# A strided-attention and feed-forward kernel on one core: fewer and finer loads at the start, and one more block of tokens in the seven-product form

## The chip, the cores and the metric

The kernel runs on one core of a Trainium2 chip, the other cores being idle. The metric is the time of one execution on the device, in microseconds (us): the median of three executions was 305.05 us (304.64 to 305.45). The profiled execution that all views below come from took 306.2 us by the same clock; its trace spans 304.4 us from the first to the last instruction. The clock that TensorE was granted is full (1.000) throughout.

Engines: TensorE multiplies matrices (PE in the profile; PEld is its loading of weights), VectorE is DVE, ScalarE is ACT, GpSimd is POOL, SyncE is SP. GpSimd issues the loads, because these also convert float32 to float16; SyncE issues stores and the transposes that are done by DMA.

## The reference, cut to what matters

```python
q, k, v: (8, 8, 576, 64)            # batch, heads, positions, head dimension
scores = (1 / 8) * q @ k.T          # for each batch and head
rel = pos[:, None] - pos[None, :]
mask = (0 <= rel < 32)                        # heads 0 to 3, "local"
mask = (rel >= 0) & (rel % 32 == 0)           # heads 4 to 7, "strided"
attn = softmax(where(mask, scores, -1e9))
x = (attn @ v) as (4608, 512)       # tokens x (heads * head dimension)
h = x @ w_in                        # w_in (512, 2048)
g = s * relu(h) ** 2 + b
out = g @ w_out                     # w_out (2048, 512), out float32
```

A local head needs only bands of 96 positions with the 32 before them, a strided head only 72 x 72 squares of eight interleaved classes each, so the attention is small. The two feed-forward products are large: 4608 x 512 x 2048 and 4608 x 2048 x 512.

## The kernel before

The program is fully unrolled. While it is being built, a small planner (`Plan`) keeps a clock of its own, with estimated durations and landing times, and picks for TensorE at each moment the next piece of work that it believes ready: a step of the attention, of the first feed-forward product (`ff1`), or of the second (`ff2`). The engines then execute in that order and wait on semaphores where reality is later than the plan. Estimates therefore change nothing but the order.

```python
LAT = {"A": 70.0, "V": 70.0, "P": 70.0, "D": 12000.0, "X": 7000.0, "Y": 12000.0}  # ns, added to an end
...                                        # A, V, P: ACT, DVE, POOL;  D, X, Y: transposes and stores by DMA

def load_vl(b):                            # v of the four local heads of batch b
    vl = v_loc[b % NV]
    for h in range(4):
        nc.gpsimd.dma_start(out=vl[LPAD:128, h, :, 0:D], in_=v_band(b, h))

def load_w_in():                           # pieces of 512, 512 and 1024 columns
    wv = moe_w_in.rearrange("(c p) f -> p c f", p=128)
    for i, at in enumerate((0, 512, 1024)):
        nc.gpsimd.dma_start(out=w_in_sb[i], in_=wv[:, :, at:at + w_in_sb[i].shape[2]])
...
def mu(eng):                               # division by the sum of the softmax, after P times v
    if eng == "A":
        for i in range(per):               # per = 6 (local) or 4 (strided)
            nc.scalar.activation(out=st["x"][:, j0 + i, 64 * e:64 * e + 64],
                                 in_=st["pa", e, j][0:nq, i, 0:D], func=AF.Copy,
                                 scale=st["rec", e, j][0:nq, i])
        return
    nc.vector.tensor_tensor(out=st["x"][:, j0:j0 + per, 64 * e:64 * e + 64],
                            in0=..., in1=..., op=ALU.mult)
...
def trans(name, j, group): ...             # q and k of a pair of heads transposed on TensorE (L429, L437)
x_by_dma = b >= 2 if loc else XS_DMA <= b < B - 1    # else x is transposed on TensorE (xtrans, L662)
...
def ff1(T, ft, ct, ...):                   # block T of 512 tokens: 16 ft x 4 ct matmuls of 512 columns (L907)
    needs.append(("w_in", ft // 4))        # relu to u on ACT or DVE, then square to gT

def ff2(T, ts, ft, ...):                   # plain form: 4 ts x 16 ft matmuls of 512 columns (L965)
    needs=[("g", T, ft), ("w_out", ft // 4)]

def ff2_seven(T):                          # T >= SEVEN = 3: seven products of 16 matmuls, 256 columns (L875)
    ...                                    # sums of quarters of gT on DVE (L747), quarters of w_out
                                           # combined once (w_mix), results joined on DVE (L794, L806, L817)
...
def second(eng):                           # everything of batch 1, after w_in, on GpSimd's queue
    fetch_qk(1)
    load_vl(1)
    ...
    early_v(1)                             # v of the strided heads
    weights_out(range(4))                  # w_out in four pieces
...
def keep_running(until):                   # matmuls on a tile of ones where the plan has nothing ready
    ghz = 1.2 if plan.t < 6000 else 2.4    # (L1201)
```

The seven-product form takes a block's 512 x 2048 times 2048 x 512 as a 2 x 2 by 2 x 2 product of quarters: seven products of quarters instead of eight, with additions in exchange. Blocks 0 to 2 take the plain form, blocks 3 to 8 the seven-product form.

Of the kernel before, what the change touches and what calls it, by code (L numbers as in the profile page):

```python
# [15 lines left out]
class Plan:  # L16
# [7 lines left out]
    LAT = {"A": 70.0, "V": 70.0, "P": 70.0, "D": 12000.0, "X": 7000.0, "Y": 12000.0}  # L24
# [92 lines left out]
class Step:  # L117
    def __init__(self, fn, ns, needs=(), group=None, keys=(), posts=(), after=None):
        self.fn, self.ns, self.needs, self.group = fn, ns, needs, group
        self.keys, self.posts, self.after = keys, posts, after  # L120
# [3 lines left out]
def kernel(  # L124
# [32 lines left out]
    for p in range(SQ):  # L157
        for c in range(SQ):
# [30 lines left out]
               for i, n in enumerate((512, 512, 1024))]  # L189
# [123 lines left out]
    def load_vl(b):  # L313
        vl = v_loc[b % NV]
        for h in range(4):
            nc.gpsimd.dma_start(out=vl[LPAD:128, h, :, 0:D], in_=v_band(b, h))  # L316
# [8 lines left out]
    def load_w_in():  # L325
        wv = moe_w_in.rearrange("(c p) f -> p c f", p=128)
        for i, at in enumerate((0, 512, 1024)):
            nc.gpsimd.dma_start(out=w_in_sb[i], in_=wv[:, :, at:at + w_in_sb[i].shape[2]])
# [80 lines left out]
    def pair_steps(b, m):  # L409
# [10 lines left out]
        def trans(name, j, group):  # L420
            alone = loc and b < HEAD_T

            def f():
                if j == 0:
                    st["p" + name] = bank(group).bitcast(FP16)[:, 0:S]
                if alone:
                    for e in range(2):
# [12 lines left out]
            s = Step(f, 70 if alone else 35, needs=[("in", name + sfx, b, mm)],  # L440
                     group=group if j == 0 else None)
            if j == nt - 1:
                key = ("t", name, id_)
                s.keys = [key]
                if name == "q":
# [14 lines left out]
                    s.posts = [([key], {"A": 1190, "V": 1440 if loc else 918}, g,  # L460
# [17 lines left out]
        x_by_dma = b >= 2 if loc else XS_DMA <= b < B - 1  # L478
# [128 lines left out]
        def av(e, j, group):  # L607
# [13 lines left out]
            if j % per == per - 1:  # L621
# [10 lines left out]
                def mu(eng):  # L632
                    if eng == "A":
                        for i in range(per):
# [12 lines left out]
                                                 **({"A": 225.0 * per} if b == 0 else {})}, mu,  # L647
# [67 lines left out]
    SEVEN = 3  # L715
# [45 lines left out]
    def mix_post():  # L761

        wl, wr = [[w_out_sb[:, H * j:H * j + H, 256 * k:256 * k + 256] for j in range(2)]
                  for k in range(2)]
        jobs = ((3, wr[1], wr[0]), (1, wr[0], wl[0]), (2, wr[1], w_mix[1]), (4, wl[1], w_mix[2]))
        before = [("F2", SEVEN - 1)]
        for i, x, y in jobs:
            plan.post(before, {"V": 1250.0},
                      lambda eng, i=i, x=x, y=y: nc.vector.tensor_tensor(
                          out=w_mix[i], in0=x, in1=y, op=ALU.subtract), [("w_mix", i)])  # L770
            before = [("w_mix", i)]
        plan.post([("ev", SEVEN - 1, ts) for ts in range(4)], {"V": 350.0},
                  lambda eng: nc.vector.tensor_tensor(
                      out=bcs[:, 256:512], in0=bcs[:, 256:512], in1=bcs[:, 0:256],
                      op=ALU.subtract), [("dbc",)])
# [121 lines left out]
    def ff1(T, ft, ct, group, cts=(0, 1, 2, 3), early=False):  # L897
        tok0 = T * PS
        def f():
            if ft == 0 and ct == cts[0]:  # L900
                gts[T] = gp.tile([128, NFT, PS], FP16, tag="gT", name="gT")
            if ct == cts[0]:
                gts["h", T, ft] = bank(group)
            at = tok0 % (NX * S)
            n = min(PS, NX * S - at)
            for lo, hi in ((0, n), (n, PS))[:1 + (n < PS)]:
                nc.tensor.matmul(  # L907
                    out=gts["h", T, ft][:, lo:hi],
                    lhsT=w_in_sb[min(ft // 4, 2)][:, ct].rearrange(
                        "p (c x l) -> p c l x", x=128, l=4)[:, max(ft // 4 - 2, 0), ft % 4],  # L910
                    rhs=xT[ct][:, (at + lo) % (NX * S):(at + lo) % (NX * S) + hi - lo],
                    start=(ct == cts[0] and lo == 0), stop=(ct == cts[-1] and hi == PS))
# [109 lines left out]
    def landing(cost):  # L1022

        nonlocal ring
        ring = max(ring, plan.t + 2000.0) + cost

        return ring + (6000.0 if plan.t > 60000.0 else 600.0)
# [4 lines left out]
    def fetch_qk(b):  # L1032
# [6 lines left out]
        for name in ("q", "k"):  # L1039
# [3 lines left out]
            if b < HEAD_T:  # L1043
                arrive(both(name + "l", b), landing(1500))
                continue
            plan.done["raw", name, b] = landing(1700 if b > 1 else 1450)
            for mm in range(2):
                pair_post(b, name, mm, ("raw", name, b))
        for name in ("qs", "ks"):
            arrive(both(name, b), landing(2000 if b > 1 else 1750))  # L1050
# [12 lines left out]
    def early_v(b):  # L1063
# [3 lines left out]
        plan.done["raw", "v", False, b] = landing(1800)  # L1067
# [5 lines left out]
    def after_landing(i, src):  # L1073
# [7 lines left out]
    AT = {"ql0": 5700.0, "kl0": 6800.0, "ql1": 7900.0, "kl1": 8900.0, "qs": 10100.0,  # L1081
          "ks": 11600.0, "vs": 13600.0, "vl0": 7100.0, "vl1": 14700.0}
# [5 lines left out]
    after_landing(0, loaded[0, "ql"][0:1, NL // 2:NL // 2 + 1])  # L1088
# [4 lines left out]
    def weights_in(eng):  # L1093
# [5 lines left out]
        for keys, cost in ([0], 2700), ([1], 2500), ([2, 3], 5000):  # L1099
# [12 lines left out]
    def second(eng):  # L1112
# [3 lines left out]
        plan.done["raw", "vl", 1] = landing(3200)  # L1116
# [5 lines left out]
    plan.post(both("vl", 0) + both("vs", 0) + [("w",)], {"P": 14000.0}, second, [("free",)])  # L1122
# [12 lines left out]
    for b in range(B):  # L1135
        for m in range(4):
            steps, last_av = pair_steps(b, m)
            att.append(steps)
            if b + 2 < B:

                if m == 0:
# [7 lines left out]
                    [("fetch", b + 2)] + both("vs", b), {"P": 3600.0}, lambda eng: fetch_v(b + 2),  # L1149
# [3 lines left out]
    for T in range(NBLK):  # L1153
# [26 lines left out]
        for ts in range(4):  # L1180

            parts = 2 if T == NBLK - 1 and ts == 3 else 1
            for part in range(parts):
                gr = Group("f2", F2B)
                for ft in range(NFT):
                    f2.append(ff2(T, ts, ft, gr, part, parts))
                    f2[-1].pos = T + 0.25 + (ts + (part + ft / NFT) / parts) / 4
    def keep_running(until):

        ghz = 1.2 if plan.t < 6000 else 2.4  # L1190
# [26 lines left out]
    while i2 < len(f2) or any(at_i[p] < len(att[p]) for p in range(len(att))):  # L1217
# [5 lines left out]
        active = [p for p in range(first, min(first + 4, len(att))) if at_i[p] < len(att[p])]  # L1223
        for p in active:
# [67 lines left out]
```

## Time and profile before

| | |
|---|---|
| median of three executions | 305.05 us |
| span of the trace | 304.4 us |
| TensorE, DVE, ACT, POOL busy | 97%, 71%, 60%, 33% of the span |
| start of `ff1` of blocks 0, 1, 2, 3 | 18.97, 56.98, 90.76, 116.84 us |
| first matmul of `ff2` of block 0, last matmul of all | 40.81, 301.0 us |

A line of the groups gives the source line, the engine and operation, the tiles out<-in with shape and count, then busy us and mean ns of one, then the idle time just before. A line of the stages ("A:B ...") gives, for each engine, busy us and number of instructions, then TensorE's clock, the share of the DMA engines and GB/s. A line of the timeline gives start, length, engine, line, and in brackets how long the engine had been idle and what ended that. Landing times of single transfers are those of the trace, too.

### The profile page before, as it was taken

What the parts mean: (1) busy time and instruction counts of PE and PEld (TensorE: products, weight loads), DVE (VectorE), ACT (ScalarE), POOL (GpSimd) and SP (SyncE); (2) the same over time, 40 slices, a digit from 0 to 9 for tenths busy, and PEclk for the clock granted to TensorE, in tenths of its full rate; (3) what the DMA queues carried; (4) which work ended last, traced back from release to release, by engine and by line L of the source; (5) the groups of instructions that cost most, each with busy time, mean ns of one, the idle gap of its engine ahead of it and who ended that gap; (6) DMA issues with size and microseconds to landing.
All of it is one profiled execution on the core that took longest, in us unless ns stands there. A gap on an engine that the chain in (4) does not pass through costs nothing.

```text
span 304.4 us, 6800 instructions
## 1 busy us (share of the span) xinstructions
PE 296.4 (97%) x2674; PEld 205.8 (68%) x2674; DVE 216.6 (71%) x474; ACT 183.9 (60%) x330; POOL 99.3 (33%) x146
## 2 busy tenths in 40 slices
PE   8998999999999999999999999999999999999995
PEld 3764655666555568767567776778888666766784
DVE  6665897698966688737997698777765366737563
ACT  2966963898747677478585946695725445445300
POOL 8771753930961095029502961200000000000000
PEclk9999999999999999999999999999999999999999
DMA  8999999999999699999999999944010200300123
GB/s 136 183 201 202 137 213 190 179 198 149 83 160 165 98 100 149 132 186 147 142 153 172 142 160 159 155 105 131 14 37 34 72 34 0 106 0 2 69 82 126
DMA packets 100826, 37.29 MB, mean 122 GB/s; under 512 B 80907, under 2 KB 97803, under 8 KB 100795
## 3 DMA queue, kind: packets, MB, share of 16 engines
q0 software_dynamic: 57232, 18.08, 60.1%
q1 hardware_dynamic: 43562, 18.78, 33.3%
q8 instruction: 21, 0.34, 0.5%
q14 instruction: 11, 0.08, 0.1%
HBM read 36.86 MB, written 10.32 MB: 155 GB/s over the span
## 4 chain that ended last, share of the span: by engine, by line
PE 83%; DMA 8%; DVE 3%; POOL 3%; issue 1%; ACT 1%; POOLq 0%
PE ps_f L907 36%; PE ps_f L875 20%; PE ps_f L965 12%; DMA kl<-in_k_dram 5%; PE ps_s L557 3%; PE ps_a L614 3%; DMA vs<-in_v_dram 2%; PE ps_s L875 2%; DMA xT<-x_dram 1%; PE ps_t L875 1%; PE ps_s L965 1%; PE ps_t L614 1%; PE ps_t L662 1%; PE ps_t L437 1%; PE ps_f L437 1%
## 5 line engine op out<-in xcount | busy, mean ns | idle before, releaser
L907 PE MATMUL ps_f<-xT,w_in_sb 128*128 128x512 f16 (+4 forms) x696 | 148.1, 340 | 0.0
L934 ACT ACTIVATE u<-ps_f 128x512 f16<-128x512 f32 x137 | 80.8, 595 | 72.6 <-PE ps_f L907 69.9
L907 PEld LDWEIGHTS <-w_in_sb 128*128 128x128 f16 x704 | 71.7, 113 | 33.1 <-DMA w_in_sb<-in_moe_w_in_dram 0.5
L875 PEld LDWEIGHTS <-gT 128*128 128x128 f16 x512 | 49.0, 98 | 12.5 <-issue 0.4
L965 PE MATMUL ps_f<-w_out_sb,gT 128*128 128x512 f16 x176 | 47.6, 379 | 0.0
L875 PE MATMUL ps_f<-w_out_sb,gT 128*128 128x256 f16 x312 | 44.2, 273 | 0.3 <-DVE o L806 0.3
L944 DVE TENSOR_TENSOR gT<-u 128x1024 f16<-128x1024 f16 x46 | 32.1, 697 | 15.1 <-ACT u L934 14.4
L942 ACT ACTIVATE gT<-u 128x1024 f16<-128x1024 f16 x26 | 27.5, 1057 | 0.7
L640 DVE TENSOR_TENSOR x_nat<-ps_a,rec 72x256 f16<-72x256 f32 (+1 forms) x55 | 25.3, 459 | 0.9
L316 POOL DMA_DIRECT2D v_loc<-in_v_dram x28 | 20.7, 759 | 14.3 <-DMA w_in_sb<-in_moe_w_in_dram 6.0
L965 PEld LDWEIGHTS <-gT 128*128 128x128 f16 x192 | 17.0, 98 | 11.1
L575 ACT ACTIVATE p_str<-ps_s 72x432 f16<-72x432 f32 (+1 forms) x45 | 20.1, 481 | 4.7 <-PE ps_s L557 4.6
L575 ACT ACTIVATE p_loc<-ps_s 128x384 f16<-128x384 f32 x46 | 20.8, 494 | 2.2 <-PE ps_s L557 1.8
L614 PEld LDWEIGHTS <-p_str 72*128 72x128 f16 x256 | 15.3, 98 | 7.3 <-issue 0.4
L747 DVE TENSOR_TENSOR gT<-gT 128x1024 f16<-128x1024 f16 x28 | 18.5, 683 | 1.4 <-ACT gT L942 1.3
L875 PE MATMUL ps_f<-w_mix,gT 128*128 128x256 f16 x144 | 19.3, 273 | 0.0
L875 PEld LDWEIGHTS <-S 128*128 128x128 f16 x160 | 15.5, 98 | 3.7
L629 DVE RECIPROCAL rec<-ps_a 72x4 f32<-72x4 f32 (+1 forms) x55 | 9.7, 177 | 11.2 <-PE ps_a L614 11.0
L321 POOL DMA_DIRECT2D v_str<-in_v_dram x16 | 13.0, 816 | 9.6 <-PE ps_f L907 5.6
L583 DVE TENSOR_TENSOR p_loc<-p_loc,masks 128x1152 f16<-128x1152 f16 x14 | 10.5, 750 | 7.6 <-ACT p_loc L575 7.4
L875 PE MATMUL ps_f<-w_mix,S 128*128 128x256 f16 x96 | 13.4, 273 | 0.0
L976 DVE SCALAR_TENSOR_TENSOR o<-ps_f,s_sb,bcs 128x512 f32<-128x512 f32 x11 | 8.2, 749 | 6.4 <-PE ps_f L965 6.2
(162 smaller groups left out, 413.2 us busy)
## 6 DMA issues: line engine op xcount, KB each, us to landing
out_dram<-o SPq DMA_DIRECT2D x34, 256.0 KB, 3.4
w_out_sb<-in_moe_w_out_dram POOLq DMA_DIRECT2D x4, 512.0 KB, 9.4
v_loc<-in_v_dram POOLq DMA_DIRECT2D x28, 72.0 KB, 8.5
qs<-in_q_dram POOLq DMA_DIRECT2D x6, 288.0 KB, 6.6
ks<-in_k_dram POOLq DMA_DIRECT2D x6, 288.0 KB, 8.0
ql<-in_q_dram POOLq DMA_DIRECT2D x5, 288.0 KB, 9.7
kl<-in_k_dram POOLq DMA_DIRECT2D x16, 72.0 KB, 3.8
v_str<-in_v_dram POOLq DMA_DIRECT2D x16, 72.0 KB, 9.9
```

The source lines that it names most:

```text
L316: nc.gpsimd.dma_start(out=vl[LPAD:128, h, :, 0:D], in_=v_band(b, h))
L321: nc.gpsimd.dma_start(out=vs[:, h, :, 0:D], in_=v[b, 4 + h].rearrange("(p j) d -> p j d", j=ST))
L575: nc.scalar.activation(out=st["pw", g][0:nk, 0:2 * n * nq], in_=st["s", g][0:nk, 0:2 * n * nq], func=AF.Exp, scale=scale)
L614: nc.tensor.matmul(out=st["a"][:, j % per, :], lhsT=st["pw", g][0:nk, i * nq:i * nq + WIDE], rhs=vt[0:nk, 2 * mm + e, j, :])
L640: nc.vector.tensor_tensor(out=st["x"][:, j0:j0 + per, 64 * e:64 * e + 64], in0=st["pa", e, j][0:nq, 0:per, 0:D], in1=st["rec", e, j][0:nq, ...
L747: nc.vector.tensor_tensor(out=at(out), in0=at(x), in1=at(y), op=op)
L875: nc.tensor.matmul(out=gts[name, T, t][:, 0] if halves else gts[name, T][:, t], lhsT=lhs(k, t), rhs=rhs(k), start=fresh and k == 0 and (ha ...
L907: nc.tensor.matmul(out=gts["h", T, ft][:, lo:hi], lhsT=w_in_sb[min(ft // 4, 2)][:, ct].rearrange("p (c x l) -> p c l x", x=128, l=4)[:, ma ...
L934: nc.scalar.activation(out=u, in_=gts["h", T, ft], func=AF.Relu)
L942: nc.scalar.activation(out=g, in_=u, func=AF.Square)
L944: nc.vector.tensor_tensor(out=g, in0=u, in1=u, op=ALU.mult)
L965: nc.tensor.matmul(out=gts[id_], lhsT=gts[T][:, ft, ts * 128:(ts + 1) * 128], rhs=w_out_sb[:, ft, cols], start=(ft == 0), stop=(ft == NFT ...
```

## The change

Its parts, by what they are for:

- **Loads.** `load_vl` brings v of the four local heads in one transfer instead of four, so that GpSimd issues fewer; w_in comes in four pieces of 512 columns, so that the last half needn't land whole before it is used.
- **First batch.** The planner's table of landing times (`AT`) and other estimates for the first two batches are replaced by others; its clock starts at 1850 ns; transposes of batch 0 that have begun go first (`sticky`); the second half of the first v is requested when the first piece of q lands, not the second.
- **Seven products from block 2 on** (`SEVEN` 3 to 2). The combinations of w_out are formed in another order, so that three of the four can be formed before block 1 is done.
- **Divisions on ScalarE** become a choice for every batch, not for batch 0 alone.
- **Last batch.** The strided heads' x of batch 7 is transposed by DMA too.
- **Estimates** of transposes by DMA and of later landings are lowered (`LAT`, `landing`).

The diff, cut to its core:

```diff
-    LAT = {"A": 70.0, "V": 70.0, "P": 70.0, "D": 12000.0, "X": 7000.0, "Y": 12000.0}
+    LAT = {"A": 70.0, "V": 70.0, "P": 70.0, "D": 10000.0, "X": 6500.0, "Y": 6000.0}
...
-               for i, n in enumerate((512, 512, 1024))]
+               for i, n in enumerate((512, 512, 512, 512))]
...
     def load_vl(b):
-        vl = v_loc[b % NV]
-        for h in range(4):
-            nc.gpsimd.dma_start(out=vl[LPAD:128, h, :, 0:D], in_=v_band(b, h))
+        nc.gpsimd.dma_start(
+            out=v_loc[b % NV].rearrange("p h t d -> p (h t) d")[LPAD:128, :, 0:D],
+            in_=v.rearrange("b h (t p) d -> b p (h t) d", p=LQ)[b, :, 0:4 * LT])
...
-            s = Step(f, 70 if alone else 35, needs=[("in", name + sfx, b, mm)],
+            s = Step(f, 40 if alone else 35, needs=[("in", name + sfx, b, mm)],
                      group=group if j == 0 else None)
+            s.sticky = b == 0 and j > 0
...
-        x_by_dma = b >= 2 if loc else XS_DMA <= b < B - 1
+        x_by_dma = b >= 2 if loc else XS_DMA <= b
...
-                                                 **({"A": 225.0 * per} if b == 0 else {})}, mu,
+                                                 "A": 260.0 * per}, mu,
...
-    SEVEN = 3
+    SEVEN = 2
...
-        jobs = ((3, wr[1], wr[0]), (1, wr[0], wl[0]), (2, wr[1], w_mix[1]), (4, wl[1], w_mix[2]))
-        before = [("F2", SEVEN - 1)]
+        early = [("bcs",)] + ([("F2", SEVEN - 2)] if SEVEN > 1 else [])
+        jobs = ((3, wr[1], wr[0], ALU.subtract, early), (2, w_mix[3], wl[0], ALU.add, []),
+                (4, wl[1], w_mix[2], ALU.subtract, []),
+                (1, wr[0], wl[0], ALU.subtract, [("F2", SEVEN - 1)]))
...
-        return ring + (6000.0 if plan.t > 60000.0 else 600.0)
+        return ring + (3500.0 if plan.t > 60000.0 else 600.0)
...
-    AT = {"ql0": 5700.0, "kl0": 6800.0, "ql1": 7900.0, "kl1": 8900.0, "qs": 10100.0,
-          "ks": 11600.0, "vs": 13600.0, "vl0": 7100.0, "vl1": 14700.0}
+    AT = {"ql0": 5200.0, "kl0": 6500.0, "ql1": 7750.0, "kl1": 8550.0, "qs": 10150.0,
+          "ks": 11650.0, "vs": 13400.0, "vl0": 7100.0, "vl1": 12000.0}
...
-    after_landing(0, loaded[0, "ql"][0:1, NL // 2:NL // 2 + 1])
+    after_landing(0, loaded[0, "ql"][0:1, 0:1])
...
-        for keys, cost in ([0], 2700), ([1], 2500), ([2, 3], 5000):
+        for keys, cost in ([0], 2700), ([1], 2500), ([2], 2500), ([3], 2500):
...
-    plan.post(both("vl", 0) + both("vs", 0) + [("w",)], {"P": 14000.0}, second, [("free",)])
+    plan.post(both("vl", 0) + both("vs", 0) + [("w",)], {"P": 12500.0}, second, [("free",)])
...
+    plan.t = 1850.0
+
     def keep_running(until):
-        ghz = 1.2 if plan.t < 6000 else 2.4
+        ghz = 1.2 if plan.t < 6400 else 2.4
...
+        active.sort(key=lambda p: not att[p][at_i[p]].sticky)
```

Left out are further estimates of the same kind (landings of q, k and v of batch 1, durations of two copies, GpSimd's time for a load) and the renaming that four pieces of w_in need in `ff1`.

## The prediction

> **What bounds the kernel now.** I read the page first, engine shares and the row of slices:
>
> ```profile
> PE 296.4 (97%) x2674; PEld 205.8 (68%) x2674; DVE 216.6 (71%) x474; ACT 183.9 (60%) x330; POOL 99.3 (33%) x146
> ...
> PE   8998999999999999999999999999999999999995
> ...
> DMA  8999999999999699999999999944010200300123
> ...
> L965 PE MATMUL ps_f<-w_out_sb,gT 128*128 128x512 f16 x176 | 47.6, 379 | 0.0
> ```
>
> TensorE is full in nearly every slice. But the last line shows why that share can't be taken as it stands: one 512-column matmul is said to last 379 ns. In the timeline the same matmuls *start* every 215 to 216 ns, so records overlap and small gaps hide behind them. I therefore took the start-to-start steps from the trace: 215.7 ns for 512 columns (L907, L965), 109.3 ns for 256 (L875), 32 ns for a 72-column transpose (L662). Summing what every step exceeds its form's usual step, I find 1.4 to 2.4 us in each ten us up to 50 (part of it an artefact of transposes that run in pairs), then about 0.1 us in each ten us up to the end, with one exception of 0.47 us at 177. So there are two regimes: up to about 57 us the order of landings decides; after it TensorE is simply full, and only fewer columns help. By stages:
>
> ```profile
> 18.90:26.90 8.00, 7.88 (x47) 4.14 (x47) 4.56 (x8) 5.09 (x11) 1.96 (x5) 1.00 1.18 208
> 26.90:31.30 4.40, 2.34 (x35) 1.24 (x36) 2.02 (x3) 2.89 (x4) 1.44 (x2) 1.00 1.54 190
> 31.30:40.80 9.50, 9.50 (x120) 6.59 (x121) 8.65 (x19) 8.53 (x19) 8.34 (x12) 1.00 1.23 158
> ...
> 57.00:150.00 93.00, 93.00 (x812) 59.60 (x811) 68.90 (x169) 66.91 (x125) 44.04 (x63) 1.00 1.28 144
> ```
>
> The hole is in the second row. The list of waits names it:
>
> ```profile
> PE ps_t L429 <- DMA ql<-in_q_dram: 1.4, 1, 1.4
> ...
> PE ps_t L429 <- DMA kl<-in_k_dram: 0.6, 1, 0.6
> ```
>
> and TensorE's timeline shows what stood before it in order:
>
> ```profile
> 23.00 4.05 PE L907 MATMUL ps_f<-xT,w_in_sb 128*128 128x512 f16 x18
> 28.49 0.45 PE L429 MATMUL ps_t<-ident,ql 96*64 96x96 f16 x12 [1.44 <-DMA ql<-in_q_dram]
> ```
>
> By start-to-start steps these two holes are 1.61 and 0.78 us. At 26.9 exactly half of block 0's first product was done, 32 of 64 matmuls. The other half needs the 1024-column piece of w_in, which landed at 26.60; the plan put q of batch 1 first, and it landed at 28.44. On GpSimd's queue:
>
> ```profile
> 22.06 0.75 POOL L316 DMA_DIRECT2D v_loc<-in_v_dram  x1 [1.96 <-DMA w_in_sb<-in_moe_w_in_dram]
> 26.89 0.72 POOL L316 DMA_DIRECT2D v_loc<-in_v_dram  x1 [4.08 <-DMA w_in_sb<-in_moe_w_in_dram]
> 28.73 0.73 POOL L316 DMA_DIRECT2D v_loc<-in_v_dram  x1 [1.11 <-DMA ql<-in_q_dram]
> 31.47 0.72 POOL L316 DMA_DIRECT2D v_loc<-in_v_dram  x1 [2.01 <-DMA kl<-in_k_dram]
> ```
>
> Each of the four v transfers is held until the transfer eight issues earlier has landed (w_in at 21.49 and 26.60, ql at 28.44, kl at 31.18). So w_out goes out only at 33.63; its first piece lands at 40.16, and the second product of block 0 starts at 40.81.
>
> **What the Trainium skill says.** "TensorE: Matmul & The Clock Gate", section "Back-to-back issue gap", gives N/2.4 + 2.5 ns, thus 215.8 and 109.2 ns for 512 and 256 columns; the trace agrees with 215.7 and 109.3. "Perfetto Trace Analysis", section "Identifying the Most-Contended Engine", calls matmul busy time a bad measure because matmuls are pipelined; here 379 against 215.7 ns. "DMA: Bandwidth & Descriptors", section "Rules for kernel authors", says to coalesce many small transfers, while its section "Why small descriptors are slow (HBM only)" puts the cost on each descriptor. A v row arrives as 128 bytes, whether in one transfer or four. The trace agrees that these are slow: between 32 and 34 us, while they arrive, 70 GB/s move, against 199 to 218 from 18 to 30. Thus I credit the merged transfer with its issues, not its bytes.
>
> **The change, part by part.**
>
> *Seven products for block 2.* Removed: 64 matmuls x 215.7 ns = 13.80 us. Added: 112 x 109.3 = 12.24 us. TensorE saves 1.56 us, in the regime where it is full, so all of it counts. DVE pays: 8 sums x 0.683 (row L747) = 5.5 us, and 7 joins x 0.75 + 0.69 against 4 x 0.75 plain ones, +2.9 us; together +8.4 us. The four combinations of w_out only move earlier. DVE was busy 28.8 of 40 us from 110 to 150, where block 2's second product now lies; 37 of 40 would be too tight.
>
> *Divisions on ScalarE.* This is what the choice is for: a division costs DVE 0.414 us (strided) or 0.546 us (local), and ACT some 0.9 to 1.35 us (12 small ones took 2.7 us, 0.225 each). ACT was busy 27.6 of those 40 us. Moving about ten divisions brings DVE back to some 32 of 40. Worth nothing by itself on TensorE; it protects the 1.56 us.
>
> *Batch 7's x by DMA.* Removed: 16 transposes x 32 ns = 0.51 us of TensorE, and two copies. Batch 7 was done near 219 us, and block 7, the first that needs it together with batch 6, started at 236.99, so a round trip through DRAM of some 15 us in the plan is covered. All 0.51 us counts.
>
> *w_in in four pieces, better estimates, merged v.* At a landing pace of 2.6 us a piece (18.93 to 21.49 for the second) the third piece should land near 24.1 and the fourth near 26.6. TensorE needs 16 x 0.2157 = 3.45 us for what one piece feeds. It thus stays behind the landings from 18.9 on and never waits for w_in; the holes of 1.61 and 0.78 us get filled with the second half of `ff1`. One 512-column matmul on ones at 20.4 (0.4 us) goes as well. What of batch 0's attention ran after 18.97 (transposes of x, some 0.8 us) can lie before, as v's second half is requested about 2.5 us earlier. Sum of what could be gained: 1.61 + 0.78 + 0.4 + 0.8 = 3.6 us. Work up to `ff2` of block 0 would then end near 40.8 - 3.6 = 37.2.
>
> But `ff2` needs w_out, and DMA is the limit here. v of batch 1 is now one issue that can leave after the third piece of w_in, and v strided and w_out follow without three more holds. I estimate the first piece of w_out 1 to 1.5 us earlier, at 38.7 to 39.2: the bytes ahead of it are the same, and only the thin stretch around 32 us can be closed. Attention of batch 1 fills part of the remaining one to two us. I credit 2.5 of the 3.6 us.
>
> *The first 6 us.* The planner's clock starting at 1850 ns removes about five 427 ns matmuls on ones, so the first transposes can start at 5.3 rather than 6.37. I give nothing for this: `ff1` cannot start before w_in lands, at 18.93, and its request waits for q of the strided heads (landed 10.15), which doesn't move.
>
> *Lower estimates for DMA* remove no work. They move steps of TensorE nearer to the true landings. The plan allowed 12 us for a transpose by DMA that landed after 2.6 to 10.6; I subtract 0.5 us of new waits.
>
> Sum: 1.56 + 0.51 + 2.5 - 0.5 = 4.07 us. 305.05 - 4.07 = 301.0 us.
>
> **The rivals.** *w_out takes the place of the wait for q.* For it: the DMA row is 8 or 9 from the start to slice 25, so moving TensorE ahead only brings it to the next landing sooner. Against it: attention of batch 1 is at hand, and DMA has a thin stretch to close. If w_out doesn't move at all, the start gives some 1 us, and the time is 302.5.
>
> *DVE becomes the bound at block 2.* For: it was busy 9.5 of 10 us from 150 to 160 already. Against: ACT has room, and block 3 ran the same form in 149 to 177 with only 0.47 us lost. If it happens, the 1.56 us are lost and the time is 302.6 or more.
>
> *Plan too optimistic.* Two transposes of x through DRAM landed at 167.3 and 173.2, and block 5 started at 179.1; with 6 us less in the plan it might be placed at about 173, right at the landing. If each of five blocks waited 0.5 us, the time would be 303.
>
> *All goes well*: the whole 3.6 us, half a microsecond from the early start, no new waits: 305.05 - 1.56 - 0.51 - 4.1 = 298.9.
>
> **Range and chances.** The two savings in columns, 2.07 us, are nearly certain; the start is the uncertain term, between 1 and 4 us, less 0 to 2 us of new waits. That gives 299.2 to 303.2 for 8 in 10. 2% of 305.05 is 6.1 us; faster than 298.95 needs everything: 0.09. Slower by that much would need a stall of over 10 us: 0.02. Within 2%: 0.89.
>
> **What would show it.** The seven-product step: L965 at 128 matmuls instead of 192, L875 at 784 instead of 672, still 109 ns apart, and no waits of TensorE on DVE between 110 and 150. Divisions: L635 on ACT after 57 us. Batch 7: L662 at 88 instead of 104. The start: no wait on ql or kl of batch 1; `ff1` of block 0 in one run from about 18.9; `ff2` starting at 38.5 to 39.2, with any hole before it ended by w_out; block 1 starting near 54.5. The optimistic plan: waits of TensorE on transposes by DMA after 100 us. The prediction is wrong if w_in's first piece moves from 18.9, if `ff2` of block 0 still starts after 40, or if TensorE loses over 1 us after 60.

## The result, and the profile after

The changed kernel takes 313.92 us (median of four executions, 313.09 to 314.86), beside 304.85 us for the kernel before on the same chip: the ratio is 1.0296, with a 95% interval of 1.0262 to 1.0331. It is 9 us slower, where the prediction had it 4 us faster. The profiled execution took 313.09 us; its trace spans 311.0 us, against 304.4 before. (The spans differ by 6.5 us and not by 9.1: the profiled execution was the fastest of four after, and before it took 306.2 us, over its median.)

First the page of the kernel after: busy times, then the row of TensorE in 40 slices of 7.8 us, its granted clock and the DMA engines, then one group of matmuls and the loads of v; the last line is that of the kernel before.

```profile
PE 296.5 (95%) x2703; PEld 211.3 (68%) x2703; DVE 218.2 (70%) x470; ACT 200.0 (64%) x400; POOL 86.0 (28%) x122
...
PE   6999999999999999999958999899999999999994
...
PEclk9799999999999999999996999999999999999998
DMA  8999999997999799999999999814310210200213
...
L968 PE MATMUL ps_f<-w_out_sb,gT 128*128 128x512 f16 x112 | 29.9, 379 | 0.6 <-DVE u L939 0.6
...
v_loc<-in_v_dram POOLq DMA_DIRECT2D x7, 288.0 KB, 12.4
...
v_loc<-in_v_dram POOLq DMA_DIRECT2D x28, 72.0 KB, 8.5
```

The busy time of TensorE is the same as before to 0.1 us, which means nothing here, as the records overlap. The row of slices says more: one large hole, a 5 and an 8 in slices 21 and 22 (155.5 to 171 us), with a 6 for the clock in the second of them. One hole of some microseconds near 160 us, then, in a stretch in which the kernel before was full. The 8 in slice 26 is a smaller one. (The 7 of the clock in slice 2 is 3.4 us of half clock from 8.6 to 12.0.) The last two lines give the median time from issue to landing of v's loads: 12.4 us, and 8.5 for the four smaller transfers of before.

By stages (columns: length, busy time of PE, PEld, DVE, ACT and POOL with their instructions, granted clock, DMA share, GB/s), of the kernel after:

```profile
26.90:31.30 4.40, 4.40 (x42) 2.22 (x41) 2.02 (x4) 3.57 (x7) 1.58 (x3) 1.00 1.68 188
...
57.00:150.00 93.00, 93.00 (x875) 65.22 (x874) 75.95 (x174) 77.51 (x167) 35.86 (x50) 1.00 1.46 140
160.00:170.00 10.00, 5.71 (x35) 3.86 (x35) 3.60 (x7) 3.87 (x8) 1.76 (x4) 0.66 1.16 194
```

and the last of these stretches in the kernel before:

```profile
160.00:170.00 10.00, 10.00 (x79) 7.61 (x78) 5.76 (x10) 6.24 (x13) 4.78 (x9) 1.00 1.14 171
```

The hole at 26.9 to 31.3, on which most of the prediction's working was spent, is closed: TensorE is busy for all of the 4.40 us, against 2.34. The block with more work for VectorE, 57 to 150, is full. What is lost is lost at 160 to 170: 35 matmuls instead of 79, and a mean clock of 0.66. TensorE's waits of the kernel after (in total, how many, longest):

```profile
PE ps_s L558 <- DMA kT_loc<-kl: 4.7, 1, 4.7
PE ps_a L429 <- DMA kl<-in_k_dram: 1.2, 1, 1.2
...
PE ps_s L558 <- DMA kT_alt<-kl: 0.7, 1, 0.7
PE ps_t L429 <- DMA ql<-in_q_dram: 0.6, 1, 0.6
```

(those on kl and ql are batch 0's, at 6.9 and 5.0 us), and its timeline around the longest:

```profile
159.32 0.27 PE L879 MATMUL ps_f<-w_mix,gT 128*128 128x256 f16 x1
164.29 0.82 PE L558 MATMUL ps_s<-qD_loc,kT_loc 128*128 128x192 f16 x4 [4.70 <-DMA kT_loc<-kl]
164.91 0.64 PE L879 MATMUL ps_f<-w_mix,gT 128*128 128x256 f16 x2
165.34 1.06 PE L911 MATMUL ps_f<-xT,w_in_sb 128*128 128x512 f16 x2
```

The scores of batch 6 (L558) stand next in TensorE's order and need the transpose of k by DMA, which lands near 164.2. Behind them stand 512-column matmuls that need nothing of it, but the order was fixed when the program was built. Then comes a second loss that no list of waits has: from 162.2 to 169.0 the trace grants half the clock, and the 512-column matmuls start every 427 ns instead of 216. The Trainium skill, page "TensorE: Matmul & The Clock Gate", Part 1, "What's actually happening", says that one idle window of about 3.4 us brings the half clock, and that one busy window is needed to leave it. Here it lasted 6.8 us, two such windows, after a wait of 4.87 us by start-to-start steps; of the 3.4 us before it TensorE was idle for 2.6, so a window need not be idle throughout.

Summing what each start-to-start step exceeds its form's usual one, as the prediction did, the stretch 150 to 170 lost 7.3 us, against 0.1 before; 190 to 210 lost 1.2 (most of it a wait for another transpose of k), against 0.1; and the end comes 4.5 us after the start of the last matmul instead of 3.5. Against these 9.3 us stand 2.1 us of columns saved, 0.3 us that TensorE is ahead at 60 us, and 0.5 us of the wait at 177 of before, which is gone. That leaves 6.4; the spans differ by 6.5.

### The profile page after: what moved, and what is told of

Same layout as the page of the kernel before. It is cut to its first block, busy times and chain, and to the rows that moved or that the text cites. A ratio compares the mean times of both kernels' runs of the same rounds, so it can differ in the third digit from the quotient of the medians.

```text
span 311.0 us, 6899 instructions
## 1 busy us (share of the span) xinstructions
PE 296.5 (95%) x2703; PEld 211.3 (68%) x2703; DVE 218.2 (70%) x470; ACT 200.0 (64%) x400; POOL 86.0 (28%) x122
## 3 DMA queue, kind: packets, MB, share of 16 engines
q1 hardware_dynamic: 45458, 19.37, 34.5%
## 4 chain that ended last, share of the span: by engine, by line
PE 72%; DMA 18%; DVE 4%; POOL 2%; issue 1%; ACT 1%; SPq 0%; POOLq 0%
PE ps_f L911 32%; PE ps_f L879 18%; PE ps_f L968 7%; DMA v_str<-in_v_dram 6%; PE ps_s L558 4%; DMA kT_alt<-kl 3%; DMA kT_loc<-kl 3%; DMA w_out_sb<-in_v_dram 3%; DMA ql<-in_q_dram 3%; PE ps_a L615 2%; PE ps_s L879 2%; PE ps_t L879 1%; PE ps_s L968 1%; PE ps_t L437 1%; POOL ql L293 1%
## 5 line engine op out<-in xcount | busy, mean ns | idle before, releaser
L879 PEld LDWEIGHTS <-gT 128*128 128x128 f16 x608 | 58.4, 98 | 13.8 <-issue 0.3
L879 PE MATMUL ps_f<-w_out_sb,gT 128*128 128x256 f16 x376 | 52.7, 272 | 0.0
L968 PE MATMUL ps_f<-w_out_sb,gT 128*128 128x512 f16 x112 | 29.9, 379 | 0.6 <-DVE u L939 0.6
L879 PE MATMUL ps_f<-w_mix,gT 128*128 128x256 f16 x176 | 25.0, 278 | 0.0
L748 DVE TENSOR_TENSOR gT<-gT 128x1024 f16<-128x1024 f16 x34 | 23.0, 699 | 1.4 <-ACT gT L945 1.3
L641 DVE TENSOR_TENSOR x_nat<-ps_a,rec 72x256 f16<-72x256 f32 (+1 forms) x46 | 21.5, 468 | 0.5
L879 PEld LDWEIGHTS <-S 128*128 128x128 f16 x176 | 17.0, 98 | 3.8
L630 DVE RECIPROCAL rec<-ps_a 72x4 f32<-72x4 f32 (+1 forms) x55 | 9.8, 178 | 12.4 <-PE ps_a L615 11.2
L558 PE MATMUL ps_s<-qD_loc,kT_loc 128*128 128x192 f16 x68 | 12.0, 265 | 4.9 <-DMA kT_loc<-kl 4.7
L1039 POOL COPY gate<-kT 1x1 f16<-1x1 f16 x6 | 1.8, 300 | 52.7 <-DMA kT<-ks 52.7
L968 PEld LDWEIGHTS <-gT 128*128 128x128 f16 x128 | 11.3, 98 | 7.3
L879 PE MATMUL ps_f<-w_mix,S 128*128 128x256 f16 x112 | 16.1, 273 | 0.0
L558 PEld LDWEIGHTS <-kT_loc 128*128 128x128 f16 x72 | 7.3, 106 | 10.4 <-DMA kT_loc<-kl 5.0
L584 DVE TENSOR_TENSOR p_loc<-p_loc,masks 128x1152 f16<-128x1152 f16 x14 | 10.4, 745 | 5.0 <-ACT p_loc L576 5.0
## 6 DMA issues: line engine op xcount, KB each, us to landing
w_in_sb<-in_moe_w_in_dram POOLq DMA_DIRECT2D x4, 512.0 KB, 10.4
v_loc<-in_v_dram POOLq DMA_DIRECT2D x7, 288.0 KB, 12.4
```

The lines of the kernel that those rows point to most:

```text
L558: nc.tensor.matmul(out=st["s", g][0:nk, c:c + 2 * nq], lhsT=(st["k"][:, i * nq:i * nq + nk] if loc else st["k"][:, i, 0:SQ]), rhs=st["q"][ ...
L584: nc.vector.tensor_tensor(out=pt[0:nk], in0=pt[0:nk], in1=mask, op=ALU.mult)
L748: nc.vector.tensor_tensor(out=at(out), in0=at(x), in1=at(y), op=op)
L879: nc.tensor.matmul(out=gts[name, T, t][:, 0] if halves else gts[name, T][:, t], lhsT=lhs(k, t), rhs=rhs(k), start=fresh and k == 0 and (ha ...
L968: nc.tensor.matmul(out=gts[id_], lhsT=gts[T][:, ft, ts * 128:(ts + 1) * 128], rhs=w_out_sb[:, ft, cols], start=(ft == 0), stop=(ft == NFT ...
```

## The experiments

Two causes were on the table. **Cause A**: the lowered estimates for DMA (`LAT`, and the 3500 ns for a landing instead of 6000) put steps of TensorE ahead of transfers that land later than that. **Cause B**: the single transfer of v lands later than four, and what follows it in the queues lands later too. Ratios are to the kernel before on the same chip, 305.8 to 306.5 us, with 95% intervals; they leave out executions over 1.5% above the fastest of their kernel, so where a variant's executions spread widely, the median of all of them is given beside the ratio.

### Four runs that make a square of the two causes

Taking back the single transfer alone, in the kernel after (the plan, and so the order, stays as it is):

```diff
-        nc.gpsimd.dma_start(
-            out=v_loc[b % NV].rearrange("p h t d -> p (h t) d")[LPAD:128, :, 0:D],
-            in_=v.rearrange("b h (t p) d -> b p (h t) d", p=LQ)[b, :, 0:4 * LT])
+        vl = v_loc[b % NV]
+        for h in range(4):
+            nc.gpsimd.dma_start(out=vl[LPAD:128, h, :, 0:D], in_=v_band(b, h))
```

> The changed kernel with v of the local heads in four transfers again; the planned order of every engine but GpSimd's issues is the same. Theory A (the lowered estimates put the scores of batch 6 on TensorE before its transposed k can have landed): the stall near 159 us stays, 4 to 5 us long and followed by half clock, time 312 to 315. Theory B (one large v transfer holds up the DMA engines, so that the transposes land late): stall under 1 us, time 303 to 306.

Taking back the landing estimate alone:

```diff
-        return ring + (3500.0 if plan.t > 60000.0 else 600.0)
+        return ring + (6000.0 if plan.t > 60000.0 else 600.0)
```

> The changed kernel with only the estimate of later landings back at +6000 (transposes keep 10000). The plan then asks for batch 6's transposes of k at 154.6 instead of 148.0 and places the scores at 166.0 instead of 159.5. Theory A: stall under 1 us, no half clock, time 303.5 to 306. Theory B: the transposes are as late after their loads as now, so the stall stays at 3 us or more, time above 310.

Both edits together:

> The changed kernel with two things undone: v in four transfers, and +6000 for later landings. If A and B together are the whole of the loss: no wait of TensorE above 1 us after 60 us, time 301.5 to 303.5, that is the 2.07 us of columns and a little of the start. If the seven-product form or the divisions have a cost of their own: above 304.

Measured, with the kernel after as the fourth corner:

| | landing estimate 3500 ns (new) | 6000 ns (old) |
|---|---|---|
| v in one transfer (new) | 1.0296 [1.0262, 1.0331] | 0.9993 [0.9968, 1.0018] |
| v in four (old) | 1.0065 [1.0036, 1.0093] | 0.9941 [0.9919, 0.9964] |

The corner at the top right and the one at the bottom left each hold one cause. Each edit takes away most of the loss (3.0% and 2.3%), and both together 3.55%: the two aren't added, they meet in the same wait. For this wait a transfer must be late *and* the plan must have counted on it early. SyncE's timeline shows the transposes of k of batch 6, first in the kernel after, then in four_v, whose order is planned alike:

```profile
154.35 4.95 SPq L490 DMA_TRANSPOSE kT_loc<-kl  x2
...
150.79 3.12 SPq L490 DMA_TRANSPOSE kT_loc<-kl  x2
```

In four_v they are issued 3.6 us sooner, and TensorE passes their scores at 158.85 without a wait. But the lower left corner looks better than its kernel is: its executions run from 305.1 to 313.9 us, with a median of 309.6, 1.2% above that of before and between the two expectations. The profile is of the fastest of them; that the longer ones stall is argued from their granted clocks (0.978 to 0.994), not seen.

The upper right corner isn't free of the wait either. Its median, 305.8 us, lies in the range expected for cause A, but its one profile is of the longest, 309.24 us, and there TensorE waits for the same transpose, 3.1 us by start-to-start steps, with 3.4 us of half clock after it:

```profile
PE ps_s L558 <- DMA kT_loc<-kl: 2.9, 1, 2.9
```

With both taken back, the rest of the change is worth something: 304.3 us, faster than before by 0.6% [0.36, 0.81], though 0.8 us above the expected range. The page of that kernel has no hole after the start and a full clock:

```profile
PE   6889999999999999999999999999999999999995
...
PEclk9999999999999999999999999999999999999999
```

### The two causes alone, in the kernel before

The single transfer put into the kernel before, whose plan it doesn't touch:

> The kernel before with the one change that v of the local heads comes in one transfer; the plan, and so the order on TensorE, is the same to the nanosecond. Theory B (the one transfer makes the 128-byte rows slow and holds up what is queued beside them): rows of batch 6's v take 17 to 19 us instead of 12.8, the transposes of its k land 2 us later than 162.0, and as the plan has some 5 us of slack there, the time rises by 0.5 to 3 us. Theory A (estimates alone): within 0.4 us of before.

The lowered estimates put into the kernel before:

```diff
-LAT = {... "D": 12000.0, "X": 7000.0, "Y": 12000.0}
+LAT = {... "D": 10000.0, "X": 6500.0, "Y": 6000.0}
-        return ring + (6000.0 if plan.t > 60000.0 else 600.0)
+        return ring + (3500.0 if plan.t > 60000.0 else 600.0)
```

> The kernel before with the lowered estimates alone (10000, 6500, 6000 and +3500); v stays in four transfers. The plan moves batch 6's scores from 167.5 to 158.5 and its transposes of k from 154.0 to 146.6. Theory A: TensorE waits on a transpose for 1 to 5 us between 155 and 200, time 306 to 310. Theory B: no wait above 1 us, time 304 to 305.

The single transfer alone gives 1.0192 [1.012, 1.0263], the estimates alone 1.010 [1.0022, 1.0178]. Both harm by themselves, and the transfer by more than expected and in another place. How it does so is to be read in two views of one_v_before, the waits of TensorE

```profile
PE ps_f L907 <- ACT u L934: 5.0, 1, 5.0
```

and ScalarE's timeline

```profile
199.36 0.73 ACT L338 COPY v_loc<-v_loc 32x640 f16<-32x640 f16 x1 [5.67 <-DMA v_loc<-in_v_dram]
```

beside the same copy in the kernel before:

```profile
193.44 0.73 ACT L338 COPY v_loc<-v_loc 32x640 f16<-32x640 f16 x1
```

The list names ScalarE's relu (`u`, L934) as what TensorE waits for. That is only the messenger: ScalarE's order is fixed, too, and its next instruction was a copy of v of batch 7, whose rows, issued at 179.53, landed at 199.33, after 19.8 us. The four transfers of before, issued from 174.19 on, landed after 6.6 to 8.1 us each, the last of them 10.4 us after the first issue. Where the list names an engine, one has to look at what that engine was waiting for.

The estimates alone leave another wait, on a transpose of the strided heads' k at 194 us:

```profile
PE ps_s L557 <- DMA kT<-ks: 2.2, 1, 2.2
```

It is followed by 3.4 us of half clock (196.7 to 200.1).

### All estimates taken back, and the early start

The kernel after with both estimates (`LAT` and landing) as before:

> The changed kernel with all the later estimates as before (+6000; 12000, 7000, 12000). Scores of batch 6 planned at 168.9. Theory A: no wait of TensorE on a transpose above 0.5 us, full clock after 12 us, and the savings in columns show: 302 to 304.5. Theory B: still a stall of 2 us or more somewhere between 150 and 200, time above 307.

and with the planner's clock starting at 0 as before, too (without `plan.t = 1850.0`, and with 6000 for 6400 in `keep_running`):

> est_old, with the planner's clock starting at 0 again and so five more matmuls on ones at the start. Theory C (fewer of them let TensorE's clock fall to half at 8.6 to 12 us, which costs the start what the loads gain): clock full from 6 us on, work done by 20 us up by 1 us, time 0.5 to 1.5 us below est_old. Rival (the start is bound by the landing of w_in and w_out, so it makes no difference): within 0.3 us of est_old.

They gave 1.0146 [1.0091, 1.020] and 1.0057 [1.0029, 1.0085]. The stall at 159 is gone in both, but est_old has another one, at 194.8:

```profile
PE ps_f L911 <- ACT u L937: 4.4, 1, 4.4
...
197.56 1.35 ACT L338 COPY v_loc<-v_loc 32x640 f16<-32x640 f16 x2 [5.87 <-DMA v_loc<-in_v_dram]
```

That is the pattern of one_v_before, and est_old_warm has it too, with 1.8 us at 194.5. So with v in one transfer, careful estimates are not a cure; which of the loads the plan happens to need next decides. The difference between the two runs suggested a third cause, that the early start leaves TensorE slow or badly placed. It was tried where nothing stalls, on the kernel with four transfers and the old landing estimate:

> four_land with the planner's clock starting at 0 again, so five more matmuls on ones at the start. Theory C: clock full from about 6 us, time 0.5 to 1.2 us below four_land. Rival (w_in and w_out bind the start): within 0.3 us.

It measured 0.9941 [0.9916, 0.9966], the same as with the early start. No cost of the early start is seen there. But the profile of that kernel has none of the half clock at 8.6 to 12.0 us that the changed kernel's has, and what that costs was not separated.

### Why a merged transfer lands late

Two transfers of two heads each, in the kernel before:

```diff
-        for h in range(4):
-            nc.gpsimd.dma_start(out=vl[LPAD:128, h, :, 0:D], in_=v_band(b, h))
+        for h in (0, 2):
+            nc.gpsimd.dma_start(
+                out=v_loc[b % NV].rearrange("p h t d -> p (h t) d")[LPAD:128, h * LT:(h + 2) * LT, 0:D],
+                in_=v.rearrange("b h (t p) d -> b p (h t) d", p=LQ)[b, :, h * LT:(h + 2) * LT])
```

> The kernel before with each band's v in two transfers of 144 KB instead of four of 72 KB; nothing else differs, and the plan is the same. Cause B as stated (the larger the single transfer, the later it lands, and ScalarE's copy of v into the padded rows then holds everything behind it): the v of batch 7 lands 11 to 15 us after its issue (four: 6.6 to 8.1; one: 19.8), the wait of ScalarE for it at 193 to 200 us is 0 to 3 us, and the ratio to before lies between, 1.002 to 1.012. Rival 1 (any merging lets all of a batch's loads queue at once, and that alone is what delays them): the same as one transfer, 1.015 to 1.022. Rival 2 (there are some us of slack, and two transfers stay inside it): 0.998 to 1.002.

1.0041 [1.0004, 1.0078], between four and one. Then four transfers again, cut by partitions instead of by head (`[b, 24 * g:24 * g + 24, 0:4 * LT]` for g in 0 to 3), and the single transfer with the strided v behind it in eight pieces instead of four:

> The kernel before with each band's v in four transfers of 72 KB again, but cut by partitions (24 partitions, all four heads) instead of by head; bytes, rows of 128 bytes, number of transfers and plan are those of before. From the first issue of a batch's v_loc to its last landing before takes 12.2 us (batch 6) and 10.4 (batch 7); two transfers take 14.6 and 14.6; one takes 17.0 and 19.8. Theory D (what counts is how much GpSimd may have outstanding: it holds the next issue while eight transfers are, so more and smaller transfers meter the loads): as before, 10 to 13 us, ratio 0.998 to 1.002. Rival E (the shape of the merged transfer, all heads of a partition one after another, is what is slow): 14 us or more, ratio 1.004 or more.

> The kernel before with each band's v_loc in one transfer of 288 KB, and the v_str behind it in eight transfers of 36 KB instead of four of 72 KB, so that GpSimd has to hold the last of them again. Theory D: the single transfer shares the engines with less, so it lands sooner than the 17.0 and 19.8 us after its issue of one transfer with four behind it, at 11 to 15, and the ratio falls from 1.0192 to 1.000 to 1.010. Rival E (the large transfer is slow in itself, whatever is queued behind): 16 us or more, ratio 1.015 to 1.03.

They gave 1.0339 [1.028, 1.0399] and 1.0034 [1.000, 1.0068]. One part of each theory stands. Making GpSimd hold the issues behind v again takes the single transfer from 1.9% to 0.3%, as theory D has it: that GpSimd holds an issue while eight transfers are outstanding is plain in before, where the third and fourth transfer of strided v leave at 148.06 and 150.35, 0.6 us after qs and ks, eight issues earlier, had landed. (Smaller pieces of strided v may help in another way, too; that was not separated.) But four transfers, held just the same, were the slowest yet when cut by partitions (1.046 by the medians of all executions), which D can't explain. As that cut might have left DMA engines out, it was tried with numbers of partitions that sixteen divides:

> The kernel before with v cut by partitions again, but into three transfers of 32 partitions (96 KB) instead of four of 24. The Trainium skill, page 'DMA: Bandwidth & Descriptors', section 'Why a DMA increments its semaphore by 16 and not by 1', says that a transfer runs on the largest number of engines up to 16 that divides its outermost dimension: that would be 12 for 24 partitions, and 16 for 32 and for the 96 of the transfers by head. If that is what made the cut of four slow (1.0339, 13.9 to 17.6 us to land): the packets of 4 bytes are back at some 6,400 instead of 11,800, and the time is between that of four and of two transfers by head, ratio 0.999 to 1.006. If the order of the rows is what is slow: as before the mend, 1.02 or more.

> The same with six transfers of 16 partitions (48 KB each). If the cut by partitions is harmless once all engines share in it, and more and smaller transfers meter the loads: v of batches 6 and 7 lands 9 to 13 us after the first issue, and the ratio is 0.996 to 1.004, the two more issues of 0.74 us per batch being off the path. If the order of the rows is what is slow: 1.02 or more.

1.020 [1.0119, 1.0281] and 1.0407 [1.0312, 1.0501]; by the medians of all executions 1.023 and 1.050. The number of 4-byte packets did go back (6,304 and 6,640, against 11,792 for the cut of 24 and 6,416 before), and the slowness stayed. In the profiles of all three cuts TensorE waits 4.9 to 5.9 us for ScalarE's relu, and ScalarE 6.5 to 8.9 us for v: the pattern of one_v_before again. The variants differ in which rows lie in one transfer:

| variant of before | transfers per batch | KB each | median us to landing | us from first issue to last landing, batches 6 and 7 | mean ns of a 128-byte packet | ratio |
|---|---|---|---|---|---|---|
| before: by head | 4 | 72 | 8.5 | 12.2, 10.4 | 38.1 | 1 |
| two heads | 2 | 144 | 11.8 | 14.6, 14.6 | 43.3 | 1.0041 |
| four heads, pieces behind it held | 1 | 288 | 14.0 | 15.0, 15.7 | 45.5 | 1.0034 |
| four heads | 1 | 288 | 16.2 | 17.0, 19.8 | 43.6 | 1.0192 |
| 32 partitions of four heads | 3 | 96 | 12.7 | 17.5, 19.7 | 49.8 | 1.0200 |
| 24 partitions of four heads | 4 | 72 | 11.9 | 19.7, 16.3 | 53.2 | 1.0339 |
| 16 partitions of four heads | 6 | 48 | 10.1 | 20.0, 16.1 | 49.4 | 1.0407 |

Not the landing of one transfer, but that of the batch's last goes with the ratio: where the longer of the two times is at most 15.7 us, the ratio is at most 1.0041, and where it is 19.7 or more, at least 1.0192.

A transfer by head reads one stretch of 147,456 contiguous bytes of DRAM (576 rows of 256 bytes in float32, each of which arrives as 128), in some order; the others read from two or four such stretches by turns, and those by partitions only 4,096 to 8,192 bytes at each of 24 places. The packets of 128 bytes (all 39,168 of GpSimd's queue, v's and others) then take 14 to 40% longer. The table is a correlation over seven kernels; what in the memory makes the scattered rows slow was not tried. Nor does the packet time alone give the order of the ratios: how many loads wait in the same queues seems to count as well, as the third and fourth rows show. All times are of one profile each; that of the last row is of an execution of 324.17 us, where the fastest took 318.67.

### Does the single transfer help at the start?

The kernel with four transfers and the old landing estimate, with one transfer for batches 0 and 1 only (`if b < 2`), and for batches 0 to 5 (`if b < 6`):

> The variant with four transfers of v and the old landing estimates (304.3 us, 0.9941 of before), with one transfer for batches 0 and 1 alone. The prediction's step on the start (fewer issues in front of w_out and of the loads behind it): the first piece of w_out lands 0.5 to 1 us sooner, the second product of block 0 starts at 38.9 to 39.4 instead of 39.84, and the time falls by 0.3 to 0.8 us: ratio 0.9915 to 0.993. If merging is neutral at the start: 0.993 to 0.995. If the merged transfer harms there too: a wait on v of batch 1 in front of block 0 or 1, and 0.996 or more.

> The same variant with one transfer for batches 0 to 5 and four for 6 and 7. If the harm lies only where the v of a batch is needed soon after its issue (batches 6 and 7, as the two stalls at 159 and 196 us say): as with one transfer at the start alone, 0.992 to 0.995. If late landing shifts the later loads through GpSimd's queue wherever it happens: 0.998 to 1.008, with a wait on a transfer at 100 to 160 us.

They gave 0.9921 [0.9895, 0.9946] and 0.9972 [0.995, 0.9994]. At the start it isn't told apart from four transfers (0.9941): the first piece of w_out is issued 1.75 us sooner (30.72 against 32.47) and lands no sooner (40.00 against 39.80). The second run lies above the first and between its two expectations. Its one profile, of one of its fastest executions (304.29 us), shows no stall after the start, so where batches 2 to 5 lose was not found. 0.9921, 303.8 us, is the best number measured here, but its lead over 0.9941 is inside the intervals.

### What the seven products for block 2 are worth

The same kernel with `SEVEN = 3`, that is, with the seven-product form only from the fourth block on, as before:

> The same variant with the seven-product form from the fourth block on, as before, instead of from the third. The prediction's step 1 (seven products in block 2 are worth 1.56 us, all of it on the path): 1.56 us slower than with them, 305.6 to 306.2 us, ratio 0.998 to 1.0005. Rival (VectorE's 8 us more work in block 2 takes it back): 0.993 to 0.996, no different from the variant with them.

1.0042 [1.0020, 1.0064], against 0.9941 with it: it is worth 1.0%, some 3 us, more than the 1.56 us predicted. By columns the difference is 1.6 us, the predicted amount; the remainder, as far as its one profile shows it, is a wait that this plan has and the other doesn't,

```profile
PE ps_s L558 <- DMA kT<-ks: 1.4, 1, 1.4
```

with smaller ones. The variant's executions spread from 305.4 to 316.0 us, with a median 0.6% above that of before. An order change shifts the time by a per cent even where nobody meant it to.

## Why the prediction was wrong

**Failed: "Lower estimates for DMA remove no work ... I subtract 0.5 us of new waits."** The first half is true, and that is all they could have been: an order with less slack. The second half was a guess: half a microsecond for the whole kernel. The wait was 4.87 us in one place, and brought half clock after it. My reason for the small number was that the transposes landed 2.6 to 10.6 us after their issue, under the old allowance of 12. But such an allowance counts from the issue, and the issue itself was late: by the planner's own clock, the transposes of k of batch 6 were requested at 148.0 and the scores placed at 159.5. In the trace they were issued from 154.35 on, behind another transpose on SyncE's queue, and TensorE was at the scores at 159.6 and stood. From that issue to the end of the wait at 164.29 it is 9.9 us, still inside the lowered allowance of 10: what the plan had wrong here was the time of the issue, by 6.3 us. In the plan of before the request came at 154.0 (in the trace 155.19) and the scores at 167.5, while the transposes landed at 161.95: 5.5 us of slack, which the prediction took for waste.

**Failed: "I credit the merged transfer with its issues, not its bytes."** It was taken for harmless, as the rows are 128 bytes in either form. The section "Rules for kernel authors" of the Trainium skill's page "DMA: Bandwidth & Descriptors", which the prediction quoted, says to coalesce many small transfers. Here coalescing four of 72 KB into one of 288 KB took v of batches 6 and 7 from 10.4 to 12.2 us (first issue to last landing) to 17.0 to 19.8, and cost 1.9% on an unchanged order. The measurement decides: what went with the loss was which rows travel together and how much was queued behind them. That a transfer lands as a whole was overlooked as well: nothing in this program uses the first head until the fourth is in, as ScalarE's copy at 199.36 in one_v_before shows.

**Failed in size: "slower would need a stall of over 10 us".** It took a stall of 4.9 us. The half clock after it cost another 2.4 us (the 7.3 us lost at 150 to 170 less the wait), a second place 1.2 us, the end 1.0 us. Also, the rival "plan too optimistic" had the right kind of wait, on transposes by DMA after 100 us, but named the wrong ones: transposes of x in front of five blocks, 0.5 us each, on which the list above has no wait. It was transposes of k in front of the scores, and nearly all in one place.

**Half right: the start, "I credit 2.5 of the 3.6 us".** The holes for q and k of batch 1 in front of the rest of `ff1` were filled, the first piece of w_out landed at 38.91 (predicted 38.7 to 39.2), `ff2` of block 0 began at 39.58 (38.5 to 39.2), block 1 at 55.66 (54.5; before 56.98). But `ff1` of block 0 began at 19.76, not 18.97, with attention's work in front of it, and `ff2` met a wait of 0.6 us on VectorE. Counted as columns done by 60 us, the kernel is ahead by 0.3 us, and by 0.9 in the variant with four transfers and the old landing estimate. Adding up holes that were closed overstated the gain, since part of the work that fills them was taken from somewhere else that was just as full; that is argued from the two sums, not tested. (The prediction's reading that DMA stands at 8 or 9 up to slice 25 passes over a 6 in slice 14; nothing rests on it.)

**Right: seven products and batch 7.** Columns fell by 2.1 us (predicted 1.56 + 0.51), L968 stands at 128 matmuls and L879 at 784, the latter start 109 ns apart, and between 110 and 150 TensorE waits for no engine. VectorE's extra work was partly taken over by the divisions on ScalarE: 72 small ones there after 57 us, against none in the kernel before, and 17 fewer on VectorE, which was busy 34.5 of the 40 us from 110 to 150 (predicted 32) and 75.95 of the 93 us from 57 to 150, against 68.90. In the variant without stalls the sum of what is left, 2.1 us of columns and 0.9 us of start, is 3.0 us; its span is 3.0 us shorter than before (301.4 against 304.4), and by the time of many executions 1.8 us.

## What to carry to other kernels

When an order is fixed while a program is built, the slack in its estimates is insurance: lower them only with the latest issue and the slowest landing of the queue in hand, and never in the same step as a change that makes landings later. Merge transfers for the number of issues only where nothing soon needs the first part, and look at the time from the first issue to the last landing, and at what is queued behind, before trusting it. A kernel whose matrix engine is full at every moment has only two things to gain or lose, fewer columns and a stall, and a stall can cost its own length and half clock after it.

## What the runs showed of the hardware that was not expected

- The half clock comes and goes on a grid of 3.41 us: every stretch of it that the eighteen traces record ahead of the last matmul lasts 3.41 or 6.83 us. It does not go by the length of the stall: one of 2.4 us (est_new_before, at 194.1) is followed by 3.4 us of half clock, another of 2.4 us (four_p_before, at 205.2) by none, those of 5.0 and 5.2 us (four_p_before, one_v_before) by 3.4 us, those of 4.5 and 4.9 us (est_old, after) by 6.8. What separates them in these traces is how long TensorE stood idle within one stretch of the grid. Counted from 60 us to 20 us before the last matmul, where the clock was full: after 2.2 to 3.4 us the next stretch was at half clock (nine cases), after at most 1.9 us never. The second stall of 2.4 us lay across two stretches, with 1.5 us in the longer part.
- Packets of 128 bytes were slower when a transfer's rows came from several places: over all packets of that size on GpSimd's queue, 35.7 to 38.9 ns in six kernels by head, 43.3 with two heads in one, 41.2 to 48.0 in six kernels with four heads in one, 49.4 to 53.2 cut by partitions.
- Cutting by 24 partitions nearly doubled the packets of 4 bytes on GpSimd's queue (11,792 against 6,416), while 32 or 16 partitions did not. The trace doesn't record the engine of a packet, so no run here shows the number of engines that three_p_before's expectation gives.
- In none of the eighteen traces did GpSimd issue a load before the one eight issues earlier had landed (1,765 issues). Whether the chip or the program's semaphores hold it was not tried.
